# A DRAM tensor of their own, and GpSimd's queue, for the first four frequencies of head 0 in a Fourier-convolution and expert kernel

## The chip, the cores and the metric

The kernel runs on one core of a Trainium2 chip. The metric is device time in microseconds (us) of one execution. The core has TensorE (PE; its weight loads are listed as PEld), VectorE (DVE), ScalarE (ACT), GpSimd (POOL) and SyncE (SP). Three of them issue DMAs in this kernel: SP, ACT and POOL. The transfers of the three queues all run on the core's 16 DMA engines.

## The reference

The reference computes two stages one after the other. The first is a long convolution of `u = x * v` (4 batches, 11456 positions, 128 channels) with a filter that a small network makes from position embeddings. It is done through a Fourier transform, and multiplied by `x` again:

```
h_filt = (maximum(pos_emb @ w1, 0) @ w2) * exp(-0.01 * pos)
y      = irfft(rfft(x * v, 2S) * rfft(h_filt, 2S))[:S]
attn   = x * y
```

The second is a mixture of experts over the 45824 rows of `attn`: rows with a positive score `row @ w_skip` are given to the best of 8 experts (128 to 1024 to 128, with a relu), scaled by the gate and added to the row; the others pass through.

## The kernel before, in words

The transform is cut in two factors: 60 frequencies `k1` (K1) times 64 positions `n2` (N2). The 128 channels are cut into 4 heads of 32 (NP, DH), and 12 runs of 32 channels (NS * DH = 384 numbers) go through together.

**First phase** (`first_phase`, L292). For head 0 there are 16 steps (`First.STEPS`). A step loads `x` and `v` for 4 positions (L190, SP's queue, 768 KB), multiplies them (L197, on DVE for the first 19 steps, then on POOL), transforms over the 60 (L214, PE), copies PSUM to a buffer `xs` (L216, ACT; there are 4 of them) and stores it to the DRAM tensor `x1d[0]` (L202, ACT's queue, 120 rows of 6 KB). Between those pieces PE makes the filter and transforms it (L251, L282, L262); ACT copies it (L264) and POOL's queue stores it to `x1f` (L270, 16 stores of 720 KB).

**Frequency phase** (`freq_phase`, L325). 60 steps `n`, 15 per head, each with 4 frequencies (KS). `load(n)` (L377) issues, all on SP's queue: for head 0 the coefficients `c2` (L383, 256 KB), then the step's slice of `x1d` (L386, 768 KB in 512 pieces of 1.5 KB), then the slice of `x1f` (L387, 192 KB in 512 pieces of 384 B). The buffer has 4 slots (QX). A step transforms over n2 (L400, PE), copies to SBUF (L404, ACT), multiplies data by filter (L411 to L420, DVE), adds (L493, L494, POOL), transforms back (L435, PE), copies (L438, ACT) and stores to `zd` (L447, SP). Beside the steps of one head, the first-phase work of the next head goes on in small pieces (`others`, L350). Before its loop the phase loads steps 0, 1 and 2 (L454) and does six pieces of head 1's first-phase work (L455).

**Output phase** (`out_phase`): transforms back over the 60, multiplies by `x`, routes the rows and runs the experts, most of it after 700 us.

The order of the work on every engine is the order in which the program writes it (`manual_schedule`); the framework adds waits on semaphores where data or buffers ask for it. A transfer that reads a DRAM tensor waits for the landing of every store to the part it reads. Each of the 16 stores of a head writes 4 positions of all 60 frequencies, so each slice of 4 frequencies needs all 16 of them. A wait in a queue holds all that stands behind it.

The program makes these waits for `load(0)`: L386 waits for the stores L202 of head 0, L387 for the stores L270.

Of the kernel before, what the change touches and what calls it, by code (L numbers as in the profile page):

```python
# [12 lines left out]
F32 = mybir.dt.float32  # L13
# [11 lines left out]
K1, N2 = 60, 64  # L25
L = K1 * N2
H2 = N2 // 2
NS = NB * B
N = L * NS
NP = 4  # L30
DH = D // NP
# [18 lines left out]
KS = 4  # L50
# [105 lines left out]
class First:  # L156
# [3 lines left out]
    Q = 2  # L160
# [2 lines left out]
    ALL = NP * STEPS  # L163
    XV, US, XS = 3, 2, 4

    def __init__(self, nc, i, x1d, x1f, mc, stage):
        self.nc, self.i, self.x1d, self.x1f = nc, i, x1d, x1f
        n = self.Q * self.RUN
        at = [0]

        def piece(k):
            at[0] += k * n
            return stage[:, at[0] - k * n:at[0]]
        self.xv = [piece(2).rearrange("n (a c) -> n a c", a=2) for _ in range(self.XV)]
        self.us = [piece(1) for _ in range(self.US)]
        self.xs = [piece(2)[0:2 * K1] for _ in range(self.XS)]
        self.used = at[0]
        self.c1 = mc.tile([128, 2 * K1], F32, name="c1")
        nc.sync.dma_start(self.c1, i["c1"])
        self.loaded, self.late = 0, []  # L180
# [17 lines left out]

    def store(self):

        for dst, xs in self.late:
            self.nc.scalar.dma_start(dst, xs)  # L202
        self.late = []

    def data(self, step, pool):
        nc, Q, RUN = self.nc, self.Q, self.RUN
        h, ch = divmod(step, self.STEPS)
        u = self.us[step % self.US]
        xs = self.xs[step % self.XS].rearrange("k (m w) -> k m w", w=RUN)
        for q in range(Q):  # L210
            ps = [pool.tile([2 * K1, 512], F32, name="ps")[:, 0:RUN] for _ in range(2)]
            for p in range(2):
                rows = slice(p * 64, p * 64 + K1)
                nc.tensor.matmul(ps[p], self.c1[rows], u[rows, q * RUN:(q + 1) * RUN], start=True, stop=True)  # L214
            for p in range(2):
                nc.scalar.copy(xs[:, 2 * q + p], ps[p])  # L216
            if q < Q - 1:
                yield
        self.late.append((self.x1d[h][:, :, 2 * Q * ch:2 * Q * (ch + 1)].rearrange("k c m w -> (k c) m w"), xs))
        self.store()  # L220
        yield

# [69 lines left out]
def first_phase(tc, fi):  # L292

    with (
        tc.manual_schedule(),
        tc.tile_pool(name="fc", bufs=1) as fc,
        tc.tile_pool(name="fp", bufs=2) as fp,
        tc.tile_pool(name="fps", bufs=4, space=PSUM) as fps,
    ):
        f = fi.filt(fc, fp, fps)  # L300
        left = 0.0
        pieces = NB * 64 * H2 // 512 + 2 * NB * H2 // 4
        pace = (pieces - FLEAD) / (fi.Q * (fi.STEPS - FEND))
        next(f)
        fi.ahead(0, 1)
        next(f)
        fi.ahead(0)
        fi.mult(0)
        for _ in range(FLEAD):
            next(f)  # L310
        for step in range(fi.STEPS):
            for n, _ in enumerate(fi.data(step, fps)):
                if n == 0:
                    fi.ahead(step + 1)
                    if step < fi.STEPS - 1:
                        fi.mult(step + 1)
                left += pace
                while left >= 1:
                    left -= 1
                    next(f, None)  # L320
        for _ in f:
            pass


def freq_phase(tc, nc, i, fi, zd, c3, spare, loads):  # L325
# [9 lines left out]
    with (  # L335
# [9 lines left out]
        def c2(k, n=1):  # L345
            t, k = (spare, k) if k < HERE else (rest, k - HERE)
            return t[:, k * 128:(k + n) * 128]
# [29 lines left out]
        def load(n):  # L377
            h, k = divmod(n, PER)
            while done[0] < h * fi.STEPS * fi.Q:
                next(todo)  # L380
            ks = slice(KS * k, KS * k + KS)
            if h == 0:
                nc.sync.dma_start(c2(ks.start, KS), i["c2"][k])  # L383
            x1 = qx.tile([128, KS, (NS + NB) * DH], F32, name="x1")
            w = NB * DH
            nc.sync.dma_start(x1[:, :, 0:fi.RUN], fi.x1d[h][ks].rearrange("k c n w -> (c n) k w"))  # L386
            nc.sync.dma_start(x1[:, :, fi.RUN:], fi.x1f[ks, :, :, h * w:(h + 1) * w].rearrange("k c n w -> (c n) k w"))  # L387
            return x1

        def spread(n, j):  # L390
# [61 lines left out]
        todo = others()  # L452
        ys = {}
        xs = {n: load(n) for n in range(QX - 1)}  # L454
        for _ in range(LEAD):  # L455
            next(todo)
# [7 lines left out]
        for n in range(ALL + LAG):  # L464
            back = backer(n - LAG, ys.pop(n - LAG)) if n >= LAG else lambda lo, hi: None
            if n + QX - 1 < ALL:
                xs[n + QX - 1] = load(n + QX - 1)
# [16 lines left out]
            piece()  # L484
            back(0, 2)
            store(nc.sync if n < ALL - 4 else nc.scalar)
            if n < ALL:
                half(1)
# [10 lines left out]
            piece(ALL)  # L499
            back(2, NB)  # L500
        store(nc.scalar)


# [532 lines left out]
def out_consts(nc, i, mc):  # L1036
    wg = mc.tile([128, 32], F32, name="wg")
    nc.vector.memset(wg, 0.0)
    nc.sync.dma_start(wg[:, 0:1], i["wskip"])
    nc.sync.dma_start(wg[:, 1:1 + E], i["wgate"])  # L1040
    val = mc.tile([128, NS], F16, name="val")
    nc.sync.dma_start(val, i["val"])
    grid = mc.tile([128, PQ + PL], F16, name="grid")
    nc.sync.dma_start(grid, i["grid"])
    cols = mc.tile([E * NS, E * NS], F16, name="cols")
    nc.sync.dma_start(cols, i["cols"])
    odd = mc.tile([E * NS, E * NS], F16, name="odd")
    nc.sync.dma_start(odd, i["odd"])
    rev = mc.tile([128, E], F32, name="rev")
    nc.sync.dma_start(rev, i["rev"])  # L1050
    tri = mc.tile([128, 128], F16, name="tri")
    nc.sync.dma_start(tri, i["tri"])
    ones = mc.tile([128, 128], F16, name="ones")
    nc.vector.memset(ones, 1.0)
    bits = mc.tile([128, 2], I32, name="bits")
    nc.vector.memset(bits[:, 0:1], 5)
    nc.vector.memset(bits[:, 1:2], PL - 1)
    tiny = mc.tile([128, 1], F32, name="tiny")
    nc.vector.memset(tiny, 1e-9)
    return wg, val, grid, cols, odd, rev, tri, ones, bits, tiny  # L1060


def out_phase(tc, i, out, zd, ex, consts):
# [6 lines left out]
    with (  # L1070
# [3 lines left out]
      with (  # L1074
# [316 lines left out]
        for ch in range(NCH):  # L1391
            for blk in range(NB):
                for lag, rank, f in ((0, 0, produced), (1, 4, turn), (2, 4.9, score), (3, 2, score2), (STORE, 9, store)):
                    steps.setdefault(first(ch) + blk + lag, []).append((rank, f, (ch, blk)))
            for lag, order, f in (
                    (6, 3, choose), (7, 1, exp), (7, 4.5, count), (7, 6, counted), (7, 6, gate), (8, 4.4, total),
                    (9, -2.5, full), (9, 0.5, spreadcounts), (9, 4.4, measure), (9, 4.5, ranks),
                    (10, -2.3, measured), (10, -2, routed), (10, 4.4, lay), (11, -2, laid), (11, 3, spread), (12, 4.5, collect), (13, -3, write)):
                steps.setdefault(first(ch) + lag, []).append((order, f, (ch,)))
# [28 lines left out]
def program(tc, i, out):  # L1428
    nc = tc.nc
    x1d = [nc.dram_tensor(f"x1d{h}", (K1, 2, N2, NS * DH), F32).ap() for h in range(NP)]  # L1430
    x1f = nc.dram_tensor("x1f", (K1, 2, N2, NB * D), F32).ap()
    zd = nc.dram_tensor("zd", (2, NP, H2 * 2 * K1 + ZR, NS * DH), F32).ap()
    lists = nc.dram_tensor("lists", (ROOM // PL, PL), I32).ap()
    with tc.tile_pool(name="mc", bufs=1) as mc:
        wf = mc.tile([128, 2 * E * F], F32, name="wf")
        fi = First(nc, i, x1d, x1f, mc, wf)
        spare = wf[:, fi.used:]
        c3 = mc.tile([128, NV, 128], F32, name="c3")
        first_phase(tc, fi)
        nc.scalar.dma_start(c3, i["c3"])  # L1440
        nc.scalar.dma_start(zd.rearrange("p h r w -> (p h) r w")[:, H2 * 2 * K1:], i["none"])
        later = {}

        def prepare():

            later["ex"] = Experts(tc, i, out, lists, mc, wf)
            yield
            later["consts"] = out_consts(nc, i, mc)
            for e in range(E):
                if e % 2 == 0:  # L1450
                    yield
                later["ex"].weights(e, 0)

            for e in range(E):
                if e != 1:
                    yield
                later["ex"].weights(e, 1)
        freq_phase(tc, nc, i, fi, zd, c3, spare, prepare())
        out_phase(tc, i, out, zd, later["ex"], later["consts"])
# [55 lines left out]
```

## Time and profile before

| | |
|---|---|
| time, median of 3 runs | 1555.54 us (1553.31 to 1558.93) |
| the profiled execution's own time | 1556.24 us |
| its span, first to last instruction | 1554.5 us |
| PE busy, share of the span | 95% |
| mean granted clock of TensorE | 0.983 |

All times in the profile count from the start of the span. A row of the timeline has the start, the time taken, the engine (with a q where it is the engine's queue of instructions that issue transfers), the line, the operation, what is written and read, and in brackets how long the engine had been idle and what ended that. In the trace the tile `x1` is called `x`, and the `xs`, `us` and `xv` buffers and the first `c2` tiles are called `wf`, because they lie in that tile.

### The profile page before, as it was taken

How to read it: one execution, taken by the hardware profiler on the slowest of the kernel's cores; microseconds unless marked ns; L12 is line 12 of the kernel's file. 1: busy time of each engine (PE TensorE's matmuls, PEld its weight loads, DVE VectorE, ACT ScalarE, POOL GpSimd, SP SyncE). 2: the span in 40 equal slices, each digit the busy share in tenths (PEclk: the TensorE clock that was granted, in tenths of full speed). 3: DMA queues.
4: the chain of work that ended last, by engine and by line, in shares of the span. 5: the costliest groups of instructions: out<-in, count | busy, mean ns of one | idle time of the engine just before them, and what ended most of it. 6: DMA issues, size and time to landing. Idle time of an engine off the chain costs nothing. (4 is left out here: it accounts for less than half of the span.)

```text
span 1554.5 us, 27988 instructions
## 1 busy us (share of the span) xinstructions
PE 1477.4 (95%) x9149; PEld 902.4 (58%) x9149; DVE 1057.0 (68%) x2356; ACT 790.3 (51%) x1643; POOL 965.7 (62%) x808
## 2 busy tenths in 40 slices
PE   7994999999999999979899999999989999999997
PEld 3551344444444434434477666666667788888887
DVE  1322876777777788866876666666658877777773
ACT  4552555555555544433455454454535555556554
POOL 0100876777777766630576459528956888888765
PEclk9997999999999999989899999999999999999999
DMA  9999999999999989989877778778521111111100
GB/s 331 312 334 342 367 385 385 369 370 364 358 384 363 310 252 340 312 291 339 276 260 218 234 229 256 252 216 241 169 57 40 43 46 45 46 46 43 40 29 25
DMA packets 199289, 362.20 MB, mean 233 GB/s; under 512 B 64508, under 2 KB 138762, under 8 KB 199102
## 3 DMA queue, kind: packets, MB, share of 16 engines
q1 hardware_dynamic: 173462, 272.15, 51.9%
q10 hardware_dynamic: 10192, 52.51, 9.1%
q0 software_dynamic: 15488, 35.74, 8.4%
q8 instruction: 74, 1.21, 0.3%
q14 instruction: 73, 0.60, 0.1%
HBM read 216.89 MB, written 145.42 MB: 233 GB/s over the span
## 5 line engine op out<-in xcount | busy, mean ns | idle before, releaser
L746 POOL DMA_INDIRECT out<-o,ids x182 | 197.1, 1083 | 149.0 <-DVE o L753 112.5
L493 POOL TENSOR_TENSOR y<-y,p 128x1536 f32<-128x1536 f32 x59 | 203.6, 3450 | 98.3 <-DVE p L420 98.3
L435 PE MATMUL ps<-y,c 64*128 64x256 f32 (+1 forms) x1440 | 258.9, 490 | 3.5 <-ACT wf L216 2.7
L675 POOL DMA_INDIRECT xt<-out,ids x182 | 192.1, 1056 | 47.9 <-issue 23.5
L435 PEld LDWEIGHTS ps<-y,c 64*128 64x128 f32 x1440 | 138.6, 187 | 116.5 <-issue 83.0
L891 DVE SCALAR_TENSOR_TENSOR hh<-hp,hh 128x1024 fp32r<-128x1024 f32 (+1 forms) x124 | 150.0, 1210 | 79.2 <-ACT hh L890 79.1
L404 ACT COPY xx<-xp 128x480 f32<-128x480 f32 x240 | 112.9, 523 | 127.2 <-PE xp L400 95.1
L438 ACT COPY z<-ps 128x512 f32<-128x512 f32 x240 | 103.6, 482 | 138.3 <-PE ps L435 129.0
L890 ACT ACTIVATE hh<-hp 128x1024 fp32r<-128x1024 f32 (+1 forms) x124 | 127.6, 1029 | 90.0 <-PE hp L742 87.1
L420 DVE TENSOR_TENSOR p<-xp,xx 128x768 f32<-128x768 f32 x240 | 169.4, 748 | 0.0
L420 DVE TENSOR_TENSOR y<-xp,xx 128x1152 f32<-128x1152 f32 x120 | 162.9, 1357 | 4.1
L411 DVE TENSOR_TENSOR xx<-xp,xx 128x384 f32<-128x384 f32 x120 | 66.7, 556 | 127.0 <-ACT xx L404 127.0
L400 PE MATMUL xp<-x,wf 128*64 128x480 f32 x512 | 118.7, 586 | 21.3 <-DMA x<-x1f 17.3
L833 PEld LDWEIGHTS bank<-wd,h 128*128 128x128 f32 x896 | 104.2, 191 | 32.8 <-issue 25.9
L648 POOL MEMSET idle<- 128x512 f16 x226 | 122.4, 542 | 0.3
L216 ACT COPY wf<-ps 120x384 f32<-120x384 f32 x256 | 111.4, 501 | 21.9 <-PE ps L214 12.7
L197 POOL TENSOR_TENSOR wf<-wf 124x768 f32<-124x768 f32 x45 | 81.8, 1818 | 64.2 <-DVE xx L411 35.0
L214 PE MATMUL ps<-wf,c 60*120 60x384 f32 x512 | 118.4, 527 | 2.7 <-ACT wf L216 1.6
L626 POOL DMA_INDIRECT lists<-pl,lies x32 | 51.5, 1609 | 105.5 <-DVE step L1257 52.3
L833 PE MATMUL bank<-wd,h 128*128 128x128 f32 x896 | 114.5, 281 | 1.3 <-DVE o L753 1.3
L494 POOL TENSOR_TENSOR y<-y,p 128x768 f32<-128x768 f32 x59 | 107.2, 1817 | 4.6
L1159 PE MATMUL y<-zt,c 128*64 128x512 f32 x344 | 96.9, 632 | 10.9 <-issue 9.0
(183 smaller groups left out, 2898.7 us busy)
## 6 DMA issues: line engine op xcount, KB each, us to landing
wf<-xv SPq DMA_DIRECT2D x64, 768.0 KB
x1d<-wf ACTq DMA_DIRECT2D x64, 720.0 KB
x<-x1d SPq DMA_DIRECT2D x60, 768.0 KB
zt<-zd SPq DMA_DIRECT2D x58, 768.0 KB
zd<-z SPq DMA_DIRECT2D x108, 384.0 KB
out<-xm SPq DMA_DIRECT2D x96, 258.0 KB
ox<-xo SPq DMA_DIRECT2D x96, 256.0 KB
x1f<-fx POOLq DMA_DIRECT2D x16, 720.0 KB
```

Of the source, the lines that this page charges most:

```text
L214: nc.tensor.matmul(ps[p], self.c1[rows], u[rows, q * RUN:(q + 1) * RUN], start=True, stop=True)
L400: nc.tensor.matmul(xp[p * 64:(p + 1) * 64, c, 0:(NS + NB) * DH], c2(n % PER * KS + k)[:, c * 64:(c + 1) * 64], x1[:, k], start=True, stop= ...
L404: nc.scalar.copy(xx[:, 2 * c, 0:w], xp[:, c, 0:w])
L420: nc.vector.tensor_tensor(o[:, :, j].rearrange("p v m b d -> p v (m b) d"), v[:, :, None, s * DH:(s + 1) * DH].broadcast_to([128, NV, m, DH]),
L435: nc.tensor.matmul(zps[p], c3[r, v], yv[r, v, :, lo:hi], start=(v == 0), stop=(v == NV - 1))
L493: nc.gpsimd.tensor_tensor(y[:, :, :, 1:], y[:, :, :, 1:], p1, ALU.add)
L648: self.nc.gpsimd.memset(self.idle, 0.0)
L675: ins = nc.gpsimd.indirect_dma_start(out=xt[:, j], out_offset=None, in_=self.rows[0:have], in_offset=bass.IndirectOffsetOnAxis(ap=ids[:, j ...
L746: ins = nc.gpsimd.indirect_dma_start(out=self.rows, out_offset=bass.IndirectOffsetOnAxis(ap=ids[:, j:j + 1], axis=0), in_=o, in_offset=Non ...
L833: nc.tensor.matmul(bank[:, j * D:(j + 1) * D], h[f // nf][:, k:k + 128], wd[u][:, f * D:(f + 1) * D], start=(f == 0), stop=(f == F // 128 ...
L890: nc.scalar.activation(v[:, 0], hp, AF.Relu)
L891: nc.vector.scalar_tensor_tensor(v[:, 1], hp, 0.0, v[:, 0].bitcast(F32), ALU.max, ALU.subtract)
```

## The change

The frequencies 0 to 3 of head 0 get a DRAM tensor of their own, `x1s`. Each of the 16 stores of head 0 is cut in two: 8 rows (48 KB) go to `x1s` on GpSimd's queue, 112 rows (672 KB) to `x1d[0]` on ACT's. In `load(0)` both loads, from `x1s` and from `x1f`, go by GpSimd's queue; `c2` stays on SP's. All other heads and steps are as before.

```diff
 class First:
     def store(self):
-        for dst, xs in self.late:
-            self.nc.scalar.dma_start(dst, xs)
+        for eng, dst, xs in self.late:
+            eng.dma_start(dst, xs)
         self.late = []
     def data(self, step, pool):
...
-        self.late.append((self.x1d[h][:, :, 2 * Q * ch:2 * Q * (ch + 1)].rearrange("k c m w -> (k c) m w"), xs))
+        m = slice(2 * Q * ch, 2 * Q * (ch + 1))
+        k = KS if h == 0 else 0
+        if k:
+            self.late.append((nc.gpsimd, self.x1s[:, :, m].rearrange("k c m w -> (k c) m w"), xs[:2 * k]))
+        self.late.append((nc.scalar, self.x1d[h][k:, :, m].rearrange("k c m w -> (k c) m w"), xs[2 * k:]))
         self.store()
...
         def load(n):
...
-            nc.sync.dma_start(x1[:, :, 0:fi.RUN], fi.x1d[h][ks].rearrange("k c n w -> (c n) k w"))
-            nc.sync.dma_start(x1[:, :, fi.RUN:], fi.x1f[ks, :, :, h * w:(h + 1) * w].rearrange("k c n w -> (c n) k w"))
+            eng, src = (nc.gpsimd, fi.x1s) if n == 0 else (nc.sync, fi.x1d[h][ks])
+            eng.dma_start(x1[:, :, 0:fi.RUN], src.rearrange("k c n w -> (c n) k w"))
+            eng.dma_start(x1[:, :, fi.RUN:], fi.x1f[ks, :, :, h * w:(h + 1) * w].rearrange("k c n w -> (c n) k w"))
...
+    x1s = nc.dram_tensor("x1s", (KS, 2, N2, NS * DH), F32).ap()
```

## Rows read from the trace of the kernel before

**Rows 1.** The page, busy shares over the whole span and in 40 slices

```profile
PE 1477.4 (95%) x9149; PEld 902.4 (58%) x9149; DVE 1057.0 (68%) x2356; ACT 790.3 (51%) x1643; POOL 965.7 (62%) x808
...
PE   7994999999999999979899999999989999999997
...
DMA  9999999999999989989877778778521111111100
```

**Rows 2.** Busy time by stretch: PE, PEld, DVE, ACT, POOL; then PEclk, DMA, GB/s

```profile
110.00:120.00 10.00, 9.75 (x54) 4.81 (x50) 2.51 (x3) 6.11 (x13) 1.04 (x2) 1.00 0.95 355
120.00:130.00 10.00, 5.94 (x25) 3.04 (x24) 1.92 (x2) 4.74 (x13) 0.00 (x0) 0.90 0.95 355
130.00:140.00 10.00, 0.00 (x0) 0.00 (x0) 0.00 (x0) 1.46 (x4) 0.00 (x0) 0.50 0.93 310
140.00:150.00 10.00, 5.12 (x16) 1.69 (x16) 0.60 (x2) 0.94 (x2) 0.00 (x0) 0.58 0.96 321
150.00:160.00 10.00, 5.47 (x26) 1.74 (x25) 9.83 (x15) 4.25 (x10) 6.38 (x3) 1.00 1.04 392
160.00:170.00 10.00, 9.99 (x54) 4.33 (x56) 8.63 (x13) 5.33 (x13) 9.84 (x6) 1.00 1.05 381
```

**Rows 3.** Waits of SP's queue, 120 to 145 us: total, times, longest

```profile
SPq L386 <- DMA x1d<-wf: 18.3, 2, 15.4
SPq L387 <- DMA x1f<-fx: 3.2, 1, 3.2
```

**Rows 4.** Timeline of SP, 106 to 150 us

```profile
132.51 0.39 SPq L386 DMA_DIRECT2D x<-x1d  x1
136.33 0.37 SPq L387 DMA_DIRECT2D x<-x1f  x1
136.75 1.25 SPq L383 DMA_DIRECT2D wf<-c  x1
138.04 0.76 SPq L386 DMA_DIRECT2D x<-x1d  x1
...
145.37 2.85 SPq L190 DMA_DIRECT2D wf<-xv  x3
```

**Rows 5.** Timeline of PE, from 119 us

```profile
125.98 1.63 PE L214 MATMUL ps<-wf,c 60*120 60x384 f32 x8 [1.63 <-ACT wf L216]
...
144.88 5.17 PE L400 MATMUL xp<-x,wf 128*64 128x480 f32 x16 [17.27 <-DMA x<-x1f]
153.04 1.83 PE L400 MATMUL xp<-x,wf 128*64 128x480 f32 x8 [2.98 <-issue]
```

**Rows 6.** Timeline of POOL, 105 to 155 us

```profile
117.17 0.52 POOL L270 DMA_DIRECT2D x1f<-fx  x1 [7.88 <-ACT fx L264]
118.01 0.52 POOL L270 DMA_DIRECT2D x1f<-fx  x1 [0.32 <-ACT fx L264]
```

**Rows 7.** Timeline of ACT, 117 to 146 us

```profile
121.36 0.32 ACTq L202 DMA_DIRECT2D x1d<-wf  x1
...
129.84 1.63 ACT L216 COPY wf<-ps 120x384 f32<-120x384 f32 x4 [3.17 <-DMA x1d<-wf]
132.45 0.39 ACTq L202 DMA_DIRECT2D x1d<-wf  x1
```

**Rows 8.** The page, costliest groups: two kinds of indirect transfer issued by POOL

```profile
L746 POOL DMA_INDIRECT out<-o,ids x182 | 197.1, 1083 | 149.0 <-DVE o L753 112.5
L675 POOL DMA_INDIRECT xt<-out,ids x182 | 192.1, 1056 | 47.9 <-issue 23.5
```

**Rows 9.** Timeline of the start, where two first loads land

```profile
1.67 0.91 SPq L243 DMA_DIRECT2D post<-post  x2
...
6.42 3.75 PE L251 MATMUL fa<-post,fw 128*128 128x512 f32 x4 [6.42 <-DMA post<-post]
```

**Rows 10.** Timeline of DVE, then of POOL, from 144 us

```profile
155.01 1.41 DVE L420 TENSOR_TENSOR p<-xp,xx 128x768 f32<-128x768 f32 x2
...
153.56 3.69 POOL L197 TENSOR_TENSOR wf<-wf 124x768 f32<-124x768 f32 x2 [35.02 <-DVE xx L411]
157.20 3.47 POOL L493 TENSOR_TENSOR y<-y,p 128x1536 f32<-128x1536 f32 x1
...
177.05 1.82 POOL L197 TENSOR_TENSOR wf<-wf 124x768 f32<-124x768 f32 x1 [0.33 <-PE ps L214]
```

**Rows 11.** Waits of all engines, 150 to 270 us: total, times, longest

```profile
ACT z L438 <- DMA wf<-xv: 5.1, 3, 1.9
...
ACT wf L216 <- DMA zd<-z: 3.5, 2, 2.0
```

More of the change, by code (lines that the diff above doesn't have):

```diff
@@ L164, with __init__ @@
     XV, US, XS = 3, 2, 4
-    def __init__(self, nc, i, x1d, x1f, mc, stage):
-        self.nc, self.i, self.x1d, self.x1f = nc, i, x1d, x1f
+    def __init__(self, nc, i, x1s, x1d, x1f, mc, stage):
+        self.nc, self.i, self.x1s, self.x1d, self.x1f = nc, i, x1s, x1d, x1f
         n = self.Q * self.RUN
@@ L1435, in program @@
         wf = mc.tile([128, 2 * E * F], F32, name="wf")
-        fi = First(nc, i, x1d, x1f, mc, wf)
+        fi = First(nc, i, x1s, x1d, x1f, mc, wf)
         spare = wf[:, fi.used:]
```

## The prediction

> **What bounds the kernel now.** I read the page first. PE is busy 95% of the span and nearly every slice shows 9; the fourth slice, around 117 to 155 us, shows 4, while the DMA engines show 9 in it [rows 1]. That hole is the place that the change touches, so I cut it into stretches of 10 us. PE falls from 9.75 us busy to 5.94, then to nothing, then 5.12, while DMA stays at 0.93 to 0.96 [rows 2]. The hole is thus a wait for data, in a stretch in which the DMA engines are not idle: a transfer can only come earlier if another goes later.
>
> Next, who waits. PE's first matmul of the frequency phase begins at 144.88 after 17.27 us of idleness ended by the load from `x1f` [rows 5]. SP's queue waits 15.4 us for the last store to `x1d`, then 3.2 us for the last store to `x1f` [rows 3], and issues the two loads of step 0 at 132.51 and 136.33 [rows 4]. So there are two conditions, not one. The last `x1d` store of head 0 is issued by ACT at 121.36 [rows 7] and lands at about 132.5: 11.1 us. The last `x1f` store is issued by POOL at 118.01 [rows 6] and lands at about 136.3: 18.3 us. The later one, on the slower queue, is not removed.
>
> **The stores.** Sixteen more transfers are issued by POOL. One of POOL's stores takes it 0.52 us [rows 6]; 16 make 8.3 us over 120 us, in which POOL is busy about 1 us in 10 [rows 2]. I cost them at nothing; without that idleness they would cost 8.3 us. Bytes stay the same: 48 KB of 720 move from ACT's queue to POOL's. An `x1f` store behind an `x1s` store waits only for ACT copies that precede its own, so nothing there either.
>
> One buffer condition gets later. ACT's copies of the third step of head 1 wait for a store of four steps before and run at 129.84 [rows 7]. Part of that store will now stand in POOL's queue behind the `x1f` stores, so the copies move to about 136.3, and the ACT store behind them from 132.45 to about 138. ACT's next work needs PE's matmuls of step 0, at 144.88 or later, so 8 us cover it; if the cover went, the excess would fall on the first step.
>
> **When the first load can go.** The sixteenth `x1s` store is issued after ACT's copies, at about 121.4 [rows 7]. It stands in POOL's queue behind the `x1f` stores of 117.17 and 118.01 [rows 6]. Nothing shows such a store. From above: it lands when the store ahead of it has landed, 136.3. From below: it overtakes, and lands in the 4.75 us that a small load takes at the start of the kernel (issued at 1.67, used at 6.42 [rows 9]): about 126. I take 136.3, since the `x1f` store ahead is the nearest row. This matters less than it seems, since the load from `x1f` waits until 136.3 in either case.
>
> **The loads themselves.** On POOL an issue takes 0.52 us for 120 pieces [rows 6] and 1.06 to 1.08 us for an indirect one [rows 8]. Neither is a load of 512 pieces. By number of pieces the upper end is 0.52 x 512 / 120 = 2.2 us; the lower end is 0.52. I take 1.06, as the nearest load on POOL: `x1s` issued by 137.4, `x1f` by 138.4. From the end of issue to PE's start took 12.0 us for the `x1d` load (132.90) and 8.2 us for the `x1f` load (136.70) [rows 4, 5]. With the middle, 10.1 us, counted from 137.4, PE starts at 147.5, against 144.88: **2.6 us later**. The ends: 136.3 + 4.75 = 141.1 (3.8 us earlier), and 138.5 + 12.0 = 150.5 (5.6 later).
>
> **What SP gets.** Two issues, 0.39 and 0.37 us [rows 4], leave its queue, and `c2` of step 1 no longer stands behind both waits (136.75). Step 1's `x1d` load goes from 138.04 to about 132.5, where it moves beside the `x1s` load instead of behind it. The loads of `x` and `v` for POOL (145.37) are issued some 5 us earlier, but stand behind the same bytes, with DMA at 0.96 [rows 2]; I give them no gain.
>
> At this place the Trainium skill speaks against the change. The page "DMA: Bandwidth & Descriptors", section "Rules for kernel authors", says that spreading DMAs over SP, ACT and GpSimd doesn't help bandwidth, as all run on the same 16 engines, and saves only issue time. By it alone the change would return 0.76 us of SP's issue time and nothing else; the rows add that SP was blocked by waits too.
>
> **From PE's start to the end.** DVE ends step 0's products at 156.42, and POOL, which before had two multiplications to do, adds them from 157.20 [rows 10]: 0.78 us of a later start is absorbed there, if POOL's own first multiplication stays at 153.56. POOL then works without a gap until 177.05. That leaves 2.6 - 0.8 = 1.8 us on POOL's path and up to 2.6 on PE's; I take 2. Later, PE shows 9 in nearly all slices up to the output phase [rows 1], so the shift passes on. What could absorb it are ACT's waits for transfers, 5.1 and 3.5 us between 150 and 270 us [rows 11]; I take nothing off. TensorE's granted clock is 0.50 to 0.58 in the hole, the lower of its two levels (1.2 GHz), and 1.00 after 150 us [rows 2]; PE had been idle before, and will have been again, so this costs the same in both.
>
> **Sum.** 0 (stores) + 2 (later start) = +2 us. The profiled execution took 1556.24 us, of which 1554.5 is the span; it lies 0.7 us over the median. 1556.24 + 2 = 1558.2 for such an execution, 1555.54 + 2 = **1557.5 us** against the median.
>
> **The rivals.** *A, forecast (0.56):* as above, 1555 to 1560.2, with an upper edge beyond.
>
> *B, it gains (0.15):* POOL's last stores land sooner. The trace shows 11.1 us for ACT's and 18.3 for POOL's; if the lighter ACT stores bring POOL's to ACT's 11.1, both loads can go from about 129 and PE starts at 129.1 + 1.1 + 10.1 = 140.3: 4.6 us earlier, 1551 (1548 to 1553.5). For it: POOL's queue is the one that lags. Against: the bytes in this stretch are the same, and DMA is at 0.95. A rule of the Trainium skill would bring it about: the same page, section "Why a DMA increments its semaphore by 16 and not by 1", says that a transfer is spread over the largest number of engines up to 16 that divides its rows. By that the stores of 120 rows use 15 engines and those of 112 rows 16, with 7 rows instead of 8 on each. No row here shows the number of engines; an eighth less of ACT's 11.1 us is 1.4 us, so by rows it is a small help.
>
> *C, it loses (0.18):* POOL takes long to write the pieces of the first loads. At 2.2 us each, `x1s` is issued by 138.5 and `x1f` by 140.7; with 8.2 to 12.0 us to landing, and SP's load of step 1 (960 KB, some 2.7 us at 355 GB/s [rows 2]) now beside them, PE starts between 148.9 and 153.2, on average 6.2 us later, 5.4 after POOL's slack: 1561 (1559 to 1564). It decides from the point where POOL's issues take over 2 us each. For it: 512 pieces are over four times those of any transfer that POOL issues in rows 6. Against: the indirect ones take 1.06.
>
> *D, nothing moves (0.11):* the `x1f` wait rules in both kernels and the waits of rows 11 swallow the rest: 1555.5.
>
> **How the numbers follow.** About 0.3% (4.7 us) is what a measurement of this kernel can tell from no change: the bounds are 1550.9 and 1560.2. Faster: two thirds of B and a little of A, 0.11. Slower: two thirds of C, 0.12, and A's upper edge, 0.07: 0.19. Within: 0.70. The range 1551 to 1562.5 leaves out half of B, a third of C and a little besides, some 0.18.
>
> **What would show it.** Right: GpSimd's queue issues the `x1s` load not before 135 us, after a wait for the sixteenth `x1s` store; PE's first L400 starts at 146 to 149, still released by a load of step 0; ACT's copies of head 1's third step move to about 136. B: the `x1s` load goes before 132 and PE starts by 141. C: POOL's issue of either load takes over 2 us. D: PE starts elsewhere, but POOL's first gap is still near 177. The prediction is wrong if PE starts before 141 or after 151, or if the first phase itself ends more than 3 us away from 127.6, where PE's matmuls ahead of the hole ended [rows 5].

## The result: slower by 0.68%, and the profile after

The changed kernel takes 1569.19 us (median of 5 runs, 1562.36 to 1571.46) against 1556.44 (5 runs) for the kernel before: a ratio of 1.0068, with a 95% interval of 1.0044 to 1.0092. The ratio is taken over all the runs; the two medians alone would give 1.0082. The forecast was 1557.5 and no change that can be measured, so it is wrong. The profiled run of the changed kernel is the quickest of its five: 1562.36 us, with a span of 1560.5, 6.0 more than before. The ratio stands for 10.6 us, so this profile shows a mild case of the loss.

Where did the 6.0 us arise? The loads of step 0 and the matmuls that they release come first, since the change was about them. Lines have moved: L391 and L392 issue the two loads (L386 and L387 before), L405 is PE's first matmul of the frequency phase (L400), L266 and L268 are the filter's last matmul and its copy (L262, L264), L274 is the filter store (L270). Timeline of PE in the changed kernel (start, duration, operation, idle time before it and its releaser):

```profile
151.65 6.13 PE L405 MATMUL xp<-x,wf 128*64 128x480 f32 x16 [17.97 <-DMA x<-x1f]
159.81 2.79 PE L405 MATMUL xp<-x,wf 128*64 128x480 f32 x8 [2.02 <-issue]
```

The gap in PE is 17.97 us, against 17.27 before [rows 5]. The frequency phase starts 6.8 us later because the gap itself starts later: at 151.65 - 17.97 = 133.68 instead of 144.88 - 17.27 = 127.61. From PE's start to the end of the span the changed kernel takes 1408.9 us, the one before 1409.6. So +6.1 in the first phase, +0.7 in the gap and -0.8 behind it make the 6.0.

The gap went through the steps that were forecast. Timelines of POOL and of ACT, changed kernel:

```profile
128.40 0.52 POOL L202 DMA_DIRECT2D x1s<-wf  x1 [1.58 <-ACT wf L216]
139.03 0.81 POOL L391 DMA_DIRECT2D x<-x1s  x1 [10.11 <-DMA x1s<-wf]
139.82 0.78 POOL L392 DMA_DIRECT2D x<-x1f  x1
...
137.80 1.63 ACT L216 COPY wf<-ps 120x384 f32<-120x384 f32 x4 [5.07 <-DMA x1s<-wf]
```

POOL issues the loads in 0.81 and 0.78 us, less than the 1.06 of the forecast, and first waits 10.1 us for the sixteenth small store. ACT's copies of head 1's third step move from 129.84 [rows 7] to 137.80 and are released by a small store, as forecast; PE's start was set by the load from `x1f` and not by them.

The loss lies ahead of all this. Busy time by stretch in the changed kernel (PE, PEld, DVE, ACT, POOL; then granted clock, DMA share, GB/s):

```profile
70.00:80.00 10.00, 10.00 (x80) 5.80 (x79) 3.20 (x5) 5.62 (x12) 2.07 (x4) 1.00 0.92 300
80.00:90.00 10.00, 6.75 (x52) 3.60 (x48) 2.85 (x4) 2.42 (x5) 1.05 (x2) 0.94 0.99 343
90.00:100.00 10.00, 9.24 (x34) 4.55 (x36) 0.69 (x1) 3.38 (x7) 0.51 (x1) 0.55 0.63 236
100.00:110.00 10.00, 10.00 (x80) 5.87 (x78) 3.27 (x5) 5.52 (x12) 2.06 (x4) 1.00 0.70 196
```

The same stretches before:

```profile
80.00:90.00 10.00, 10.00 (x82) 6.09 (x78) 2.41 (x4) 5.67 (x13) 1.03 (x2) 1.00 0.95 308
90.00:100.00 10.00, 10.00 (x79) 5.68 (x79) 3.80 (x5) 4.28 (x10) 1.03 (x2) 1.00 0.96 358
100.00:110.00 10.00, 9.90 (x68) 5.28 (x66) 2.94 (x4) 5.13 (x11) 1.03 (x2) 1.00 0.99 332
```

Count the matmuls between 90 and 100 us: 34 where there were 79. PE's busy time of 9.24 us hides it: the granted clock is 0.55 there on average (0.50 is 1.2 GHz, the lower of its two levels), and a matmul takes longer (rows in the last section). And the DMA engines, near full before, fall to 0.63 and 0.70. How it came, and what followed, is seen in five timelines of the changed kernel, those of POOL, ACT, PE, DVE and SP:

```profile
73.08 1.05 POOL L274 DMA_DIRECT2D x1f<-fx  x2
...
90.12 0.59 ACT L268 COPY fx<-ps 120x512 f32<-120x512 f32 x1 [5.66 <-DMA x1f<-fx]
...
90.75 2.91 PE L266 MATMUL ps<-hw,cf 64*120 64x512 f32 x5 [4.00 <-ACT fx L268]
...
97.78 0.69 DVE L287 TENSOR_TENSOR hw<-fa,win 128x512 f32<-128x512 f32 x1 [10.47 <-PE fa L286]
102.86 0.95 DVE L197 TENSOR_TENSOR wf<-wf 124x768 f32<-124x768 f32 x1
...
87.34 0.33 SPq L190 DMA_DIRECT2D wf<-xv  x1
...
103.83 0.33 SPq L190 DMA_DIRECT2D wf<-xv  x1
```

The waits of SP's queue, 78 to 104 us (total, times, longest), first in the changed kernel, then before:

```profile
SPq L190 <- DVE wf L197: 28.7, 3, 16.1
```

```profile
SPq L190 <- DVE wf L197: 29.1, 4, 9.3
```

A pair of filter stores is issued at 73.08. ACT's copy into that buffer, free only when the second has landed, starts at 90.12 after a wait of 5.66 us; PE, whose PSUM tiles ACT has not emptied, is idle for 4.00 us, and its clock is at 0.50 for about 10 us. DVE waits 10.47 us for PE, so its next multiplication, which frees a data buffer, comes only at 102.86; SP waits 16.1 us for it with the next load, and the DMA engines run dry. Before, ACT's longest wait for a filter buffer was 2.7 us and SP's longest for DVE here 9.3; SP waited as long in total, but in four parts instead of three. ACT's waits for filter buffers in the kernel before, up to 135 us:

```profile
ACT fx L264 <- DMA x1f<-fx: 7.0, 4, 2.7
```

### The profile page after: what moved, and what is told of

It reads as the page before. It is cut to its first block, busy times and chain, and to the rows that moved or that the text cites. A ratio compares the mean times of both kernels' runs of the same rounds, so it can differ in the third digit from the quotient of the medians.

```text
span 1560.5 us, 28026 instructions
## 1 busy us (share of the span) xinstructions
PE 1483.7 (95%) x9149; PEld 904.7 (58%) x9149; DVE 1055.9 (68%) x2356; ACT 790.4 (51%) x1643; POOL 974.2 (62%) x826
## 5 line engine op out<-in xcount | busy, mean ns | idle before, releaser
L895 ACT ACTIVATE hh<-hp 128x1024 fp32r<-128x1024 f32 (+1 forms) x124 | 127.6, 1029 | 90.0 <-PE hp L747 87.9
L443 ACT COPY z<-ps 128x512 f32<-128x512 f32 x240 | 103.6, 482 | 136.1 <-PE ps L440 129.6
L405 PE MATMUL xp<-x,wf 128*64 128x480 f32 x512 | 121.1, 596 | 20.6 <-DMA x<-x1f 18.0
```

Source lines behind the costliest of these rows:

```text
L405: nc.tensor.matmul(xp[p * 64:(p + 1) * 64, c, 0:(NS + NB) * DH], c2(n % PER * KS + k)[:, c * 64:(c + 1) * 64], x1[:, k], start=True, stop= ...
L895: nc.scalar.activation(v[:, 0], hp, AF.Relu)
```

## Experiments

All ratios are against the kernel before, run beside the experiment on the same chip. The letters in the expectations stand for: S, the small stores on GpSimd's queue cost the time; L, the loads there do; C, the cut of each store into 112 and 8 rows does; O, the order in which POOL issues the stores; R, the mere number of transfers; B, the bytes of the small stores in that queue; X, the tie of the data buffers `xs` and of POOL's order to the small stores; I, small stores beside stores of 112 rows; Q, GpSimd's queue gets too little of the full DMA engines and falls behind; N, what a store of 8 rows does to single engines. "Phase end" is the start of PE's first matmul of the frequency phase less the idle time before it (it so includes the pieces of head 1 done ahead), "MB" what the DMA engines moved from 30 to 120 us, both in one profiled run:

| run | edit | ratio [interval] | phase end | MB |
|---|---|---|---|---|
| before | | 1 | 127.6 | 29.4 |
| after | the change | 1.0068 [1.0044, 1.0092] | 133.7 | 27.3 |
| e1 | after, loads on SP | 1.0068 [1.0041, 1.0096] | 138.6 | 25.3 |
| e2 | after, small stores on ACT | 1.0020 [0.9998, 1.0042] | 133.5 | 28.4 |
| e3 | after, both back | 1.0016 [0.9997, 1.0035] | 131.1 | 28.6 |
| e4 | after, 3 filter buffers | 1.0078 [1.0051, 1.0105] | 142.9 | 27.3 |
| e5 | before, 3 filter buffers | 0.9992 [0.9979, 1.0006] | 130.2 | 29.6 |
| e6 | after, half the filter stores on ACT | 1.0044 [1.0026, 1.0062] | 143.0 | 26.6 |
| e7 | before, the same | 1.0000 [0.9984, 1.0015] | 130.6 | 29.2 |
| e8 | e1 with 24 rows on GpSimd | 1.0091 [1.0059, 1.0123] | 146.3 | 25.2 |
| e9 | after, filter stores issued at once | 1.0060 [1.0030, 1.0090] | 142.8 | 26.3 |
| e10 | before + 16 stores of 512 B | 0.9960 [0.9935, 0.9985] | 135.4 | 27.5 |
| e11 | before, two pieces ahead | 1.0014 [0.9990, 1.0038] | 120.8 | 29.4 |
| e12 | before + 48 KB a step, GpSimd | 1.0054 [1.0033, 1.0075] | 137.3 | 27.1 |
| e13 | before + 512 B a step from `xs` | 0.9987 [0.9965, 1.0010] | 134.0 | 28.2 |
| e14 | before + small stores doubled | 1.0083 [1.0058, 1.0108] | 140.2 | 26.0 |
| e15 | e10 again | 1.0000 [0.9982, 1.0017] | 127.8 | 29.9 |
| e16 | before + 48 KB a step, ACT | 1.0074 [1.0050, 1.0099] | 147.0 | 26.1 |
| e17 | after, all filter stores on ACT | 1.0058 [1.0032, 1.0084] | 134.1 | 27.9 |
| e18 | before, all filter stores on ACT | 0.9968 [0.9947, 0.9989] | 129.6 | 28.5 |

The last two columns are of one execution each and scatter: e10 and e15 are the same kernel, and its phase ends at 135.4 in one profile and 127.8 in the other. The execution profiled is the quickest of its run for the changed kernel and the slowest for e4, e6 and e10 (1582.55 us, where the median of e10 is 1572.27). That profile of e10 has a stall too, 36 matmuls from 90 to 100 us at a clock of 0.70, without a small store's bytes. The verdicts therefore go by the ratios. Times of different sets don't compare: the kernel before took 1579.6 us beside e9 to e11 and 1556 to 1561 beside the others.

### Which part of the change: e1, e2, e3

e1 puts the first loads back on SP's queue:

```diff
-            eng, src = (nc.gpsimd, fi.x1s) if n == 0 else (nc.sync, fi.x1d[h][ks])
+            eng, src = (nc.sync, fi.x1s) if n == 0 else (nc.sync, fi.x1d[h][ks])
```

> The changed kernel, but both loads of step 0 go by SP's queue again; the 16 small stores stay on GpSimd's. Theory S (the small stores in GpSimd's queue make the filter's stores land later, ACT waits for the filter's buffers, PE idles and its clock falls): about 1566 to 1570 us, a ratio of 1.006 to 1.009, and the last store of head 0 issued near 128 us instead of 121.4. Theory L (the loads on GpSimd's queue cost the time): 1556 us, a ratio of 0.998 to 1.002. Theory C (any cut of the stores into 8 and 112 rows does it, whatever the queue): 1566 to 1570.

e2 puts the small stores on ACT's queue, beside the large ones; e3 does both, so that the cut alone is left:

```diff
-            self.late.append((nc.gpsimd, self.x1s[:, :, m]...
+            self.late.append((nc.scalar, self.x1s[:, :, m]...
```

> The changed kernel, but the 16 small stores go by ACT's queue; the two loads of step 0 stay on GpSimd's. Theory S: 1556 us, a ratio of 0.998 to 1.002, the last store of head 0 near 121 us. Theory L: 1566 to 1570. Theory C: 1566 to 1570.

> Only the cut: the small stores on ACT's queue, the loads on SP's. Theories S and L: 1556 us, a ratio of 0.998 to 1.002. Theory C: 1566 to 1570, a ratio of 1.006 or more.

e1 has the whole loss; e2 and e3 measure 0.20% and 0.16%, not clear of nothing, with intervals that end at 0.42% and 0.35%; those of e1 and e3 don't meet. So the small stores on GpSimd's queue make the loss, or most of it if the cut alone costs what e3's interval allows, and the loads there show no cost. e1's profile, a more typical execution than the changed kernel's, has the loss in the same place: its span is 11.2 us longer than before, and its first phase ends 11.0 later. Totals of the DMA engines from 30 to 120 us, first e1:

```profile
DMA packets 5089, 25.34 MB, mean 282 GB/s; under 512 B 888, under 2 KB 888, under 8 KB 5083
```

then e3:

```profile
DMA packets 5567, 28.62 MB, mean 318 GB/s; under 512 B 832, under 2 KB 832, under 8 KB 5561
```

then the changed kernel and the one before:

```profile
DMA packets 5574, 27.34 MB, mean 304 GB/s; under 512 B 975, under 2 KB 975, under 8 KB 5568
```

```profile
DMA packets 5603, 29.37 MB, mean 326 GB/s; under 512 B 746, under 2 KB 746, under 8 KB 5597
```

Of the nine runs with a ratio of 1.0044 or more (e1, e4, e6, e8, e9, e12, e14, e16, e17) none moves more than 27.9 MB, of the other nine only e10 moves less. In that stretch the slow kernels move less, not more. In seven of the nine the DMA engines are also less busy there, with a share of 0.84 to 0.91 against 0.94 before; in e4 and e17 they are as busy (0.94 and 0.95), and e18, which is quick, has 0.90, so the share alone doesn't part them. Busy time by stretch for the kernel before, e3 and e17 (columns as above):

```profile
30.00:120.00 90.00, 88.61 (x650) 50.55 (x648) 27.93 (x37) 46.94 (x100) 8.56 (x16) 1.00 0.94 326
```

```profile
30.00:120.00 90.00, 88.08 (x626) 50.11 (x624) 27.76 (x38) 45.32 (x96) 8.55 (x16) 1.00 0.96 318
```

```profile
30.00:120.00 90.00, 85.46 (x605) 48.31 (x604) 26.16 (x35) 43.22 (x92) 5.71 (x11) 0.98 0.95 310
```

Divide what was moved by the busy share: 326 / 0.94 = 347 GB/s before, 331 in e3, 326 in e17, 338 in the changed kernel. All twelve kernels with stores of 48 KB lie at 323 to 338, the eight without them at 341 to 352, one execution each. So the same bytes keep the engines busy longer where the small stores are, on whichever queue. That alone isn't the loss, since e2 (333) and e3 pay it too.

### Is it the wait for a filter buffer: e4 to e8

If the late landing of filter stores costs only through the two buffers, a third should heal it (e4; e5 is the control), and half of the stores on ACT's queue should halve it (e6; e7 the control). e8 asks for the dose: e1 with 16 more rows of each store in GpSimd's queue, as a second transfer there.

```diff
-            xs = [fp.tile([...], F32, name=f"fx{p}") for p in range(2)]
+            xs = [fp.tile([...], F32, name=f"fx{p}", bufs=3) for p in range(2)]
...
-                nc.gpsimd.dma_start(self.x1f[:, :, n0:n0 + M]...
+                (nc.gpsimd, nc.scalar)[p].dma_start(self.x1f[:, :, n0:n0 + M]...
...
+            self.late.append((nc.gpsimd, self.x1d[h][k:3 * k, :, m]..., xs[2 * k:6 * k]))
+            k *= 3
```

> The changed kernel with three pairs of filter buffers instead of two, so that ACT's filter copies wait for a store one pair earlier. Theory S, with the filter's buffer as the way in: the wait of ACT for the filter's stores (10.6 us in the profile of the changed kernel) goes to about 0, the last store of head 0 comes at 121 us or sooner, time 1554 to 1558. Theory L, or theory S by another way (the buffers of the data, or the plain load on the engines): still 1564 to 1570.

> The kernel before, with three pairs of filter buffers. Theory Q (the DMA engines are full in the first phase and GpSimd's queue, which carries the filter's stores, gets too little of them; it falls behind until something has to wait for its landings, and more buffers only put that off): no gain, a ratio of 0.998 to 1.005. Theory S with the filter's buffers as the way in: a gain of the kernel before too, 0.995 to 0.999, since its ACT waited 7.0 us for the filter's stores.

> The changed kernel, but every second one of the 16 filter stores (11.5 MB in all, half of it) goes by ACT's queue. Theory Q: GpSimd's queue no longer falls behind, the first phase has no stall: the last store of head 0 near 121 us or sooner, a ratio of 0.995 to 1.001. Theory N (not the share of the queue but what a small store of 8 rows does to single engines): the loss stays, 1.006 or more.

> The kernel before, with every second filter store on ACT's queue. Theory Q: the filter's stores land sooner (second of a pair 18.2 us before, then 12 or less), step 0's load goes earlier, 0.994 to 0.999. Theory N: 0.999 to 1.003.

> The kernel of e1 (small stores on GpSimd, loads on SP), with 24 rows of each store of head 0 on GpSimd's queue (8 to x1s and 16 to x1d) and 96 on ACT's. Theory Q: the more bytes change over to GpSimd's queue, the longer it lags: a ratio of 1.010 to 1.025. Theory N: 1.010 or more too, or as e1 (1.007) if it is the store's presence and not its size.

A third buffer doesn't help: 1.0078. The stall only comes later, as the timeline of ACT in e4 shows:

```profile
107.25 0.58 ACT L268 COPY fx<-ps 120x512 f32<-120x512 f32 x1 [6.28 <-DMA x1f<-fx]
```

e6 leaves 1.0044, e7 costs nothing. Three times the rows cost little more than one (1.0091 against 1.0068, overlapping), so it is not a price by the row either. Q expected no gain in e5 and got that, but no loss in e6, a gain in e7 and at least 1.010 in e8, and got none of these; N expected 1.006 or more in e6, and is neither borne out nor excluded.

### Order, number, and pieces ahead: e9, e10, e11

In the changed kernel POOL works in order, and a pair of filter stores can stand behind a small store that waits for later ACT copies. e9 issues each pair right behind its copies:

```diff
             for p in range(2):
                 nc.scalar.copy(xs[p][:, :, :, blk], ts[p])
-            yield
-            if blk < NB - 1:
-                return
-            for p in range(2):
+            for p in range(2 * (blk == NB - 1)):
                 n0 = p * H2 + ch * M
...
+            yield
```

> The changed kernel, with each pair of filter stores written into the program right behind the ACT copies that fill it, and so ahead of the next small store, instead of behind it. Theory O (in GpSimd's queue a filter store stands behind a small store that waits for later ACT copies, which holds two or three of the eight pairs back by about 1.6 us each): the loss goes, a ratio of 0.998 to 1.002. Theory R (every further transfer in GpSimd's queue costs that queue more than its bytes, in whatever order): still 1.005 to 1.009.

e10 adds to the kernel before sixteen transfers on GpSimd's queue, with hardly a byte and from a constant; e11 is the kernel before with two instead of six pieces of head 1's first-phase work done ahead of the frequency loop (`LEAD = 2`, L455).

```diff
         self.store()
+        if h == 0:
+            nc.gpsimd.dma_start(self.tiny[:, 16 * ch:16 * ch + 16], self.c1[0:8, 0:16])
```

> The kernel before, with 16 further stores of 512 bytes each (8 rows of 64 bytes, from a constant that is there from the start, to a DRAM tensor that nobody reads) on GpSimd's queue, in the places of the small stores. Theory R: the number of transfers costs, 1.004 to 1.009. Theory O, or the bytes that change queues: 0.998 to 1.002.

> The kernel before, with two pieces of head 1's first-phase work ahead of the frequency phase instead of six (LEAD), so that one store of 720 KB instead of three competes with the first loads. If the hole of 17 us is set by the DMA backlog at its start: PE starts the frequency phase 3 to 5 us sooner, 1551 to 1555 us for 1556 (0.997 to 0.9995), less what the delayed pieces cost later; if by the landing of the last filter store alone: no change or slower, 0.999 to 1.003.

e9 keeps the loss at 1.0060, so the order is not the cause. e10 came out faster, at 0.9960, outside of what either theory expected; repeated as e15 it gave 1.0000, so nothing is built on it, and the number of transfers shows no cost. e11 has PE idle from 120.8 on and its frequency phase starts at 138.78, 6.1 us sooner than before, but it is no quicker: presumably because the four pieces are only done later, which is not shown.

### Bytes, tie or company: e12 to e15

e12 adds the bytes alone, from a tile of zeros; e13 the tie alone; e14 both, with ACT's stores whole:

```diff
+        if h == 0:
+            nc.gpsimd.dma_start(self.extra[:, 1536 * ch:1536 * (ch + 1)], self.blank)      # e12
+            nc.gpsimd.dma_start(self.tiny[:, 16 * ch:16 * ch + 16], xs[0:8, 0, 0:16])      # e13
+            nc.gpsimd.dma_start(self.extra[:, 1536 * ch:1536 * (ch + 1)], xs[0:8])         # e14
```

> The kernel before, with 16 stores added on GpSimd's queue, one beside each first-head store: 8 rows of 6 KB each from a tile of zeros to a DRAM tensor that nothing reads. They are of the size and shape of the change's small stores, but wait for no ACT copy and hold no xs buffer. Theory B (the bytes): 48 KB a step more in GpSimd's queue make the filter stores behind them land late, as in the changed kernel: ratio 1.004 to 1.007, waits of ACT for the filter buffers over 8 us in the first phase, PE past its first phase at 131 to 134 us. Theory X (the tie): what costs is that an xs buffer, and POOL's order, now hang on ACT's copies and on a landing in GpSimd's queue; then this run costs nothing: 0.998 to 1.002, PE through at 126 to 129 us.

> The kernel before, with 16 stores of 512 bytes (8 rows of 64 bytes) added on GpSimd's queue, taken from xs, so that POOL waits for ACT's last copy of the step ahead of each, and the xs buffer comes free only when that store has landed too. Hardly any bytes. Theory B (the bytes): 0.997 to 1.002. Theory X (the tie): 1.004 to 1.007, with xs waits on ACT and filter stores issued late on POOL, PE through its first phase at 131 to 134 us.

> The kernel before, whose ACT stores keep all 120 rows, with 16 stores added on GpSimd's queue of the first 8 rows of xs (48 KB each) to a DRAM tensor that nothing reads: the tie and the bytes together, without the cut of ACT's stores to 112 rows. Theories B and X both: 1.005 to 1.008. Theory I (the small stores cost only beside ACT's stores of 112 rows, since the two then share out the 16 engines otherwise): 0.999 to 1.002.

> The kernel before with 16 stores of 512 bytes from a constant on GpSimd's queue once more; the first time it gave 0.996. If that was the state of one chip, the ratio is now 0.999 to 1.002; if small transfers in that queue shift the first phase to a better order, it is 0.994 to 0.998 again and the first phase ends before 126 us.

X falls: 0.9987 with the tie and no bytes. I falls: 1.0083 without the cut. B holds so far: 16 times 48 KB that nothing waits for and nothing reads cost 1.0054, with the stall of the changed kernel. Stretch of e12, then ACT's waits for filter buffers up to 135 us (total, times, longest; 7.0, 4, 2.7 before):

```profile
110.00:120.00 10.00, 10.00 (x42) 4.58 (x40) 1.56 (x2) 3.06 (x7) 0.00 (x0) 0.60 0.64 199
```

```profile
ACT fx L266 <- DMA x1f<-fx: 11.7, 4, 5.2
```

### That queue, or the bytes; and the filter stores out of it: e16, e17, e18

e12's bytes are additional, which the change's are not. e16 puts the same stores on ACT's queue:

```diff
-            nc.gpsimd.dma_start(self.extra[:, 1536 * ch:1536 * (ch + 1)], self.blank)
+            nc.scalar.dma_start(self.extra[:, 1536 * ch:1536 * (ch + 1)], self.blank)
```

> The kernel before, with the same 16 stores of 48 KB of zeros as in the run with extra bytes on GpSimd's queue (which gave 1.0054), but on ACT's queue. If 0.75 MB more of transfer in the first phase is itself the cost (768 KB at the 330 GB/s or so of that stretch are 2.3 us, a ratio of 1.0015, and more where it stalls something), this run gives 1.004 to 1.007 as well. If it is GpSimd's queue, which also carries the filter stores, this run gives 0.999 to 1.002 and no wait of ACT for a filter buffer over 4 us.

e17 (the changed kernel) and e18 (the one before) move every filter store to ACT's queue:

```diff
-                nc.gpsimd.dma_start(self.x1f[:, :, n0:n0 + M]...
+                nc.scalar.dma_start(self.x1f[:, :, n0:n0 + M]...
```

> The changed kernel with all 16 filter stores on ACT's queue, so that the small stores and the first loads are alone on GpSimd's. If the loss is made by filter stores that land late behind the small stores, it goes: 0.999 to 1.003, no wait of ACT for a filter buffer over 4 us, PE through its first phase by 130 us. If the small stores cost by themselves (their landings in GpSimd's queue, the xs buffers), it stays: 1.005 to 1.008.

> The kernel before with all 16 filter stores on ACT's queue: what this move is worth without the change, as the measure for the run with the changed kernel. Half of the move gave 1.0000, so all theories expect 0.998 to 1.003.

e16 costs 1.0074, no less than e12. So e12 doesn't speak of GpSimd's queue at all: 0.75 MB more, on either queue, cost 8 to 12 us where the rate of that stretch, 326 GB/s, would ask for 2.4, an estimate. The stall is the same one, and deeper. Stretch of e16:

```profile
110.00:120.00 10.00, 5.56 (x15) 2.23 (x16) 0.00 (x0) 3.25 (x7) 0.00 (x0) 0.50 0.46 163
```

e17 does what it was built for: ACT's waits for filter buffers shrink from 10.6 us in the changed kernel to 1.2. First the changed kernel, then e17:

```profile
ACT fx L268 <- DMA x1f<-fx: 10.6, 3, 5.7
```

```profile
ACT fx L268 <- DMA x1f<-fx: 1.2, 1, 1.2
```

Yet the time stays at 1.0058. Against its control e18, the change costs as much as ever: 1.0058 / 0.9968 = 1.009, with intervals that don't meet. But e17 does not only take a wait away, it brings another one: ACT now issues the filter stores itself, and such an issue takes up to 3.85 us. In the rows below a pair takes 3.93, and ACT's next copy starts only when it is through. Timeline of ACT in e17, then its waits for its own issues, 55 to 125 us:

```profile
98.27 3.93 ACTq L274 DMA_DIRECT2D x1f<-fx  x2
102.30 1.07 ACT L268 COPY fx<-ps 120x512 f32<-120x512 f32 x2 [4.42 <-issue]
```

```profile
ACT fx L268 <- issue: 7.2, 2, 4.4
```

PE waits for ACT's filter copies 4.5 us from 55 to 125 in e17, 5.8 in the changed kernel, 1.6 in e18 and 1.3 before. In e18 the longest such issue takes 2.04 us, so in these two profiles ACT's issues are longer where the small stores are. The path through the filter buffers, which the changed kernel's profile shows so plainly, is thus one way for the loss to reach PE, and with it closed the loss is still there. That ACT's issues are the other way is not shown: in e3 they take up to 2.49 us too, at a ratio of 1.0016. The profiles of e17 and e18 part by 4.5 us in the first phase and by 3.4 in the gap behind it (16.30 against 12.92), and by little after that.

e18 comes out under the kernel before, by 0.3% and with an interval that ends at 0.9989: filter stores on ACT's queue, without the change. It was tried in one set of runs, and 0.998 to 1.003 had been expected; e10 stood at 0.9960 in one set too, and did not repeat.

## Why the prediction was wrong

- **The stores: this step failed.** It read "I cost them at nothing", because POOL is idle nine tenths of that time and the bytes stay the same. Both reasons are true, and the step is the loss: e1, with the small stores on GpSimd's queue and the loads back on SP's, has the ratio of the change, 1.0068 or 10.6 us for a term put at 0, and with the stores on ACT's queue (e2, e3) 0.2% is left, not clear of nothing. What the step left out is the transfers themselves. The issuer's idleness covers the issue, 0.52 us, and not the transfer, and here the DMA engines are busy at about 0.95 and move less per busy share (338 GB/s against 347). The prediction used the full DMA engines against every gain in the gap and did not ask what they mean for a store moved between queues.
- **The place.** "The first phase ends more than 3 us from 127.6" was one of the two signs named for a wrong prediction; it ended at 133.7. The other, a start of PE after 151, follows from it: 151.65.
- **One buffer condition gets later: right.** 129.84 to about 136 was forecast, 137.80 came, and it cost nothing that can be seen. What releases them is right; that the time is so close is luck, since 6.1 of the 8.0 us are the lateness of the whole first phase.
- **When the first load can go, and the loads: the right steps, and a little dear.** The gap grew by 0.7 us; 2.6 were forecast. POOL's issues took 0.81 and 0.78 us, not 1.06. Two misses offset each other: the sixteenth small store landed 10.6 us after its issue (128.40 to 139.03), where 14.9 had been taken (121.4 to 136.3), and from the end of the first load's issue to PE's start it took 11.8 us instead of 10.1.
- **What SP gets: right.** No gain showed. Its `c2` of step 1 was out early, but PE's start is still set by the load from `x1f`.
- **From PE's start to the end: the size is right, the way is not.** 0.6 us of the later start were to be absorbed there (2.6 less 2); 0.8 were, in one execution of each kernel. It was to happen because POOL's first multiplication stays at 153.56; that came at 157.44, and POOL's first addition at 162.80 against 157.20.
- **The rivals.** C had the right sign by the wrong mechanism: it needed POOL's issues over 2 us. Its 1561 lies 8 us under the median. B did not occur.

The changed kernel was 4 us ahead at ACT's tenth store of head 0 (79.02 against 83.23), and lost about 11 us from there to the sixteenth. The lighter ACT stores don't explain the lead, since most of it is there at the first of them, before any store has run. ACT's first store in the changed kernel, then before:

```profile
14.73 0.35 ACTq L202 DMA_DIRECT2D x1d<-wf  x1
```

```profile
17.45 0.38 ACTq L202 DMA_DIRECT2D x1d<-wf  x1
```

In the other profiles that store goes between 14.39 (e17) and 18.24 us (e4), with and without the change.

The Trainium skill's page "DMA: Bandwidth & Descriptors", section "Rules for kernel authors", says that spreading transfers over SP, ACT and GpSimd saves issue time only. The measurement agrees that there is no gain, and goes beyond it: a loss of 0.68%. The same section says of many small transfers that those under 64 KB are mostly overhead. By that sixteen more transfers of 48 KB would cost on any queue; added ones do (e12, e16), but sixteen made by cutting, on ACT's queue, measure 0.16%, not clear of nothing (e3).

**What stays open.** Shown: the small stores on GpSimd's queue cause the loss, in the first phase. None of these makes it by itself: the first loads, the cut, POOL's order, the number of transfers, the tie to `xs`, a lack of filter buffers, filter stores in the same queue. Also shown is that this phase answers to a small added load on its DMA engines with stalls worth several times the bytes (e12, e14, e16), and the changed kernel has just such a stall. Why 48 KB a step cost next to nothing when ACT's queue carries them beside the other 672 KB (e3), and 0.7% when GpSimd's queue carries them, no run settles. Nor does a run put the small stores on SP's queue, so whether it is GpSimd's queue or any second one is open. How each store is spread over the 16 engines, and how an engine divides its time between queues, would be the next things to look at; the views used here don't show them.

## What to carry to other kernels

An idle issuing engine makes a transfer's issue free, not the transfer: in a stretch where the DMA engines are as busy as here (0.94), price a moved store by a run of its own, even when no byte is added. When a profile shows one plain chain from a late landing to the loss, break that chain in an experiment before believing it, and look at what the broken chain leaves: here the loss stayed (e17), and ACT waited for its own issues instead. In such a stretch it is worth trying large stores on one queue; here that gave 0.9968 in one set of runs (e18).

## What the runs showed of the hardware

A short stall of PE costs more than its idle time. In the changed kernel 4.00 us of idleness were followed by a granted clock of 0.50:

```profile
88.90:99.10 10.20, 8.35 (x30) 4.18 (x32) 0.69 (x1) 3.38 (x7) 0.51 (x1) 0.50 0.71 270
```

PE's matmuls by line in that stretch (count, busy time, mean ns), then from 70 to 80 us, at a granted clock of 1.00:

```profile
L266 PE MATMUL ps<-hw,cf 64*120 64x512 f32 x10 | 5.6, 1066 | 4.0 <-ACT fx L268 4.0
L214 PE MATMUL ps<-wf,c 60*120 60x384 f32 x4 | 3.0, 844 | 0.0
L286 PE MATMUL fa<-fw,h 128*64 128x128 f32 x16 | 2.0, 431 | 0.0
```

```profile
L266 PE MATMUL ps<-hw,cf 64*120 64x512 f32 x20 | 5.3, 618 | 0.0
L286 PE MATMUL fa<-fw,h 128*64 128x128 f32 x48 | 3.9, 305 | 0.0
L214 PE MATMUL ps<-wf,c 60*120 60x384 f32 x12 | 2.4, 482 | 0.0
```

At the busy time that each kind took there, the 10, 4 and 16 matmuls would have needed 4.75 us (2.65, 0.80 and 1.30) instead of 8.35: an estimate of 3.6 us more lost, so 7.6 in all.

Issues of large loads on POOL took 0.78 and 0.81 us for loads of 512 pieces, where 1.06 to 1.08 for an indirect one had been the nearest row [rows 8]. An issue on ACT's queue took 0.31 us alone, as at 79.02 in the changed kernel, and up to 3.85 where a second transfer was issued right behind another (e17).
